# Seven products moved to the front of a stage in a fused retention and feed-forward kernel

## The chip, the cores and the metric

The kernel runs on one core of a Trainium2 chip. The time is device time in microseconds (us) for one execution. Five engines work side by side, each through its own list of instructions in the order in which the program wrote them: TensorE (PE in the profile; its weight loads are PEld), VectorE (DVE), ScalarE (ACT), GpSimd (POOL) and SyncE (SP), which issues most transfers. An instruction that waits holds up all that stand behind it on its engine.

## The reference

A retention layer with a decaying state is followed by a feed-forward layer with a PReLU. In the reference's own words, cut:

```python
gamma = 1.0 - 2.0 ** (-5.0 - np.arange(H))
for t in range(S):                       # B=4, H=8, S=768, D=64
    state = gamma * state + einsum('bhd,bhe->bhde', k[:, :, t], v[:, :, t])
    y[:, :, t] = einsum('bhd,bhde->bhe', q[:, :, t], state) / sqrt(D)
x = y.transpose(0, 2, 1, 3).reshape(3072, 512)
h = x @ w_in                             # 512 x 2048
g = max(h, 0) + alpha * min(h, 0)
out = g @ w_out                          # 2048 x 512, float32
```

## The kernel before

The 3072 tokens are worked in six blocks of 512, numbered 0 to 5, each of two units of 256 tokens. A block has a retention part (scores, masks, outputs, a state handed from unit to unit), a first layer (512 features into 2048, which gives the tile `gt`) and a second layer (2048 into 512). The retention of the next block is written in between the matmuls of the second layer of the present one. Blocks 0 and 1 have first layers of their own (`ffn1`). Blocks 2, 3, 4 and 5 use `ffn1_mixed`, which the change touches.

**The stage `ffn1_mixed` (L396).** The 2048 features are 16 tiles of 128, numbered 0 to 15. Twelve of them (2 to 7 and 10 to 15) are ordinary: four matmuls of 512 columns (L409) into one PSUM bank, then an activation on ACT, `hm = relu(-h)` (L422), and a gate on DVE (L429) that forms `gt = h + (1 - alpha) * hm`. The other four (0, 1, 8 and 9) form group "a" and go through a Winograd form of Strassen's product, with seven products in place of eight. A product is four matmuls of 256 columns (L470). Products 1, 6, 7 and 4 add up in bank 4 (`hx`), products 2, 5 and 3 in bank 5 (`hy`). Between them the results are taken out:

- after product 1, ACT copies bank 4 (copy C1, L483); after product 2, DVE adds that copy to bank 5, which gives C11 (L488);
- after product 6, ACT copies bank 4 (u2); after product 7 it copies it again (u3), and DVE adds u3 to bank 5, with products 2 and 5 in it, which gives C22 (L488);
- after product 4, bank 4 holds C21, which gets one activation on ACT and two half gates of 256 columns on DVE;
- after product 3, DVE adds u2 to bank 5, which gives C12 (L488).

C11, C22 and C12 are gated elsewhere: an activation on ACT (L422, from the sum in SBUF), then a multiplication (L441) and an addition (L447) on POOL. The steps `g11a`, `g22a` and `g12a` of the order string stand for that. A step `s2:5` forms two sums on DVE (L366) over tiles 2 to 4 and 10 to 12 of `gt`, for the second layer; `s5:8` and `s0:2` do it for the rest.

The string `order` (L493) sets the program order on all engines: `n2:7` is tile 2 into bank 7, `p1a` is product 1 with what takes its result out. It is walked by a generator. The loop over the blocks (L873) ticks it: first the rescaling of the next block's q and k for one unit is written (two instructions of 128x1024 on POOL, L156, a transposing transfer and three loads on SP; in block 2 also a cast of v on POOL), then eight ticks, which are two steps of tile or product, then the same for the second unit, eight ticks more, and then the rest. Block 5 has no next block, so none of that.

The tiles `hm`, which hold an activation for the gate, come from a ring of five buffers; `os` (the sums) from a ring of three, `cu` (the copies) from one of four.

**What follows the stage.** `ffn2_seven` (L598) is the second layer, again seven products, each of 16 matmuls of 256 columns (L629). Its first product reads tiles 0 to 7 of `gt` in that order for the block's first 128 tokens, and then again for the next 128; eight ticks after its start the state sums (L219) and the scores (L272) of the next block come in. The scores write banks 4 to 7. Its third product reads the sums of L366. In block 5 nothing comes in between.

Of the kernel before, what the change touches and what calls it, by code (L numbers as in the profile page):

```python
# [21 lines left out]
def kernel(  # L22
# [373 lines left out]
    def ffn1_mixed(n):  # L396
# [89 lines left out]
        def plus(o, t):  # L486
# [4 lines left out]


        order = (  # L493
            "n2:7 n10:2 p1a n3:3 p2a n11:6 g11a p6a n4:1 p5a n12:0 s2:5 p7a n5:7 n13:2 g22a"
            " p4a n6:3 p3a n14:6 g12a n7:1 n15:7 s5:8 s0:2"
        )
        banks = {"a": (4, 5)}
        X, Y, t = {}, {}, {}
# [374 lines left out]
    for n in range(1, NBLK):  # L873
        more = n + 1 < NBLK
        u0 = 2 * (n + 1)
        if n > 1:
            gen = ffn1_mixed(n)
            if more:
                for u in (u0, u0 + 1):
                    i = rescale(G, u, 0, 0, 8)  # L880
                    if u == u0:
                        behind(i, gate)
                    i = rescale(G, u, 1, 0, 8)
                    if u == u0:
                        behind(i, xgate)
                    turn_dma(u)
                    if n == 2:
                        cast_v(G, u)
                    if u + 2 < NU:
                        load(u + 2)  # L890
                    tick(gen, 8)
            tick(gen)
# [68 lines left out]
```

## Time and profile before

| | |
|---|---|
| median of the runs | 211.59 us (211.43 to 212.95, three runs) |
| the profiled execution | 212.18 us, of it the span 210.5 us |
| PE busy | 194.6 us (92%) |
| DVE busy | 167.4 us (80%) |
| ACT busy | 109.1 us (52%) |
| POOL busy | 107.7 us (51%) |
| share of the chain that ended last | PE 57%, DVE 17%, DMA 13% |

Rows of the trace give the start in us from the span's start, the duration in us, the engine, the line of the kernel, the operation, what it writes and reads, the shapes and the count of merged instructions; brackets behind them give the idle time of the engine ahead of the row, and what ended it. Instructions of one engine overlap a little, so the distance of two starts is shorter than a duration.

### The profile page before, as it was taken

The numbers are of one execution on the slowest core, as the hardware profiler recorded it, in microseconds if no ns is written. First come the engines' busy times: TensorE is split into PE (matmuls) and PEld (weight loads), VectorE is DVE, ScalarE is ACT, GpSimd is POOL, SyncE is SP. The second block draws the span as 40 slices with busy tenths as digits, with TensorE's granted clock in tenths as the row PEclk, the third lists the DMA queues.
The fourth block names the chain that finished last, engine by engine and source line by source line (L and its number), as shares of the span: only waits on it lengthen the run. The fifth ranks groups of instructions, "written<-read, shape, count | busy, mean of one in ns | idle before, by whom it ended". The sixth has DMA issues, their size and how long they took to land.

```text
span 210.5 us, 5678 instructions
## 1 busy us (share of the span) xinstructions
PE 194.6 (92%) x2362; PEld 133.1 (63%) x2362; DVE 167.4 (80%) x278; ACT 109.1 (52%) x185; POOL 107.7 (51%) x116
## 2 busy tenths in 40 slices
PE   7789998999999999997899999799998899998993
PEld 2458444584565878554778655688654788654782
DVE  7884985666998997779997679998678997678941
ACT  2376675352666154575275476454486154476221
POOL 2488037750489354985574864573965560045200
PEclk9999999999999999999999999999999999999999
DMA  6999998999986996799411599611650011200004
GB/s 171 342 218 155 185 290 157 278 178 243 311 290 147 272 295 207 195 317 257 120 51 53 167 278 255 203 53 53 186 113 3 0 53 53 100 0 2 18 35 150
DMA packets 64697, 33.95 MB, mean 161 GB/s; under 512 B 18064, under 2 KB 64160, under 8 KB 64672
## 3 DMA queue, kind: packets, MB, share of 16 engines
q1 hardware_dynamic: 60272, 29.37, 48.3%
q0 software_dynamic: 4224, 4.19, 13.3%
q8 instruction: 18, 0.29, 0.6%
q10 hardware_dynamic: 176, 0.03, 0.2%
q14 instruction: 7, 0.06, 0.1%
HBM read 27.30 MB, written 6.29 MB: 160 GB/s over the span
## 4 chain that ended last, share of the span: by engine, by line
PE 57%; DVE 17%; DMA 13%; issue 4%; ACT 3%; POOL 2%; SPq 0%; ACTq 0%; DVEq 0%; POOLq 0%
PE ox L629 14%; PE oy L629 10%; PE hps L409 10%; DVE gt L429 8%; DMA qs<-in_q_dram 5%; PE hps L546 5%; PE ops L581 5%; DMA wout<-in_moe_w_out_dram 4%; DMA win<-in_moe_w_in_dram 4%; DVE gs L366 3%; DVE os L488 2%; ACT hm L422 2%; PE y L317 2%; PE kps L95 2%; PE hy L470 2%
## 5 line engine op out<-in xcount | busy, mean ns | idle before, releaser
L409 PE MATMUL hps<-xT,win 128*128 128x512 f16 x192 | 46.7, 379 | 0.0
L429 DVE SCALAR_TENSOR_TENSOR gt<-hm,oma,hps 128x512 f16<-128x512 f32 x48 | 35.1, 745 | 12.9 <-ACT hm L422 11.9
L422 ACT ACTIVATE hm<-hps 128x512 f32<-128x512 f32 x48 | 27.6, 594 | 15.4 <-PE hps L409 15.4
L629 PEld LDWEIGHTS <-gs 128*128 128x128 f16 x320 | 30.9, 98 | 4.3 <-DVE gs L366 0.4
L559 DVE SCALAR_TENSOR_TENSOR gt<-hm,oma,hps 128x256 f16<-128x256 f32 (+1 forms) x44 | 25.1, 599 | 6.3 <-ACT hm L557 4.4
L629 PEld LDWEIGHTS <-gt 128*128 128x128 f16 x240 | 22.7, 98 | 11.1 <-DVE gt L429 6.8
L409 PEld LDWEIGHTS <-win 128*128 128x128 f16 x192 | 18.8, 98 | 15.8
L546 PE MATMUL hps<-xT,win 128*128 128x256 f16 (+1 forms) x176 | 28.4, 321 | 0.0
L441 POOL TENSOR_TENSOR hm<-hm,oma 128x512 f32<-128x512 f32 x12 | 12.5, 1041 | 28.8 <-ACT hm L422 28.8
L156 POOL TENSOR_TENSOR kdq<-ks,tab 128x1024 f16<-128x1024 f32 (+1 forms) x10 | 17.3, 1728 | 18.6 <-DMA ks<-in_k_dram 8.6
L645 ACT ACTIVATE cu<-ox 128x512 f32<-128x512 f32 (+1 forms) x18 | 9.5, 526 | 28.3 <-PE ox L629 28.3
L557 ACT ACTIVATE hm<-hps 128x512 f32<-128x512 f32 x32 | 19.1, 597 | 9.3 <-PE hps L546 9.3
L156 POOL TENSOR_TENSOR kdq<-qs,tab 128x1024 f16<-128x1024 f32 (+1 forms) x13 | 21.2, 1634 | 5.2 <-DVE xsum L393 4.5
L546 PEld LDWEIGHTS <-win 128*128 128x128 f16 x176 | 17.1, 98 | 10.6
L245 POOL TENSOR_TENSOR tf<-ss,tab 128x256 f32<-128x256 f32 x16 | 12.2, 765 | 16.8 <-DVE ss L244 16.5
L260 POOL CAST tg<-tf 64x256 f16<-64x256 f32 x29 | 14.1, 488 | 11.3 <-DVE tf L241 9.9
L284 DVE TENSOR_TENSOR m<-sca,mi 128x512 f16<-128x512 f32 x24 | 16.4, 685 | 3.7 <-PE scb L272 3.7
L629 PE MATMUL ox<-wsum,gs 128*128 128x256 f16 x160 | 19.1, 273 | 0.1
L335 ACT ACTIVATE xT<-y 128x512 f16<-128x512 f32 x24 | 16.2, 742 | 5.0 <-PE y L317 4.9
L284 DVE TENSOR_TENSOR m<-scb,mi 128x512 f16<-128x512 f32 x24 | 16.4, 681 | 0.0
L366 DVE TENSOR_TENSOR gs<-gt 128x768 f16<-128x768 f16 (+2 forms) x18 | 16.0, 890 | 0.3
L629 PE MATMUL ox<-wout,gt 128*128 128x256 f16 x80 | 10.9, 274 | 5.7 <-DVE gt L429 5.7
(75 smaller groups left out, 307.5 us busy)
## 6 DMA issues: line engine op xcount, KB each, us to landing
out_dram<-os SPq DMA_DIRECT2D x21, 256.0 KB, 2.2
vs<-in_v_dram SPq DMA_DIRECT2D x10, 512.0 KB, 6.6
ks<-in_k_dram SPq DMA_DIRECT2D x8, 512.0 KB, 4.6
qs<-in_q_dram SPq DMA_DIRECT2D x8, 512.0 KB, 5.8
ks<-in_k_dram SPq DMA_DIRECT2D x8, 256.0 KB, 4.5
qs<-in_q_dram SPq DMA_DIRECT2D x8, 256.0 KB, 4.6
win<-in_moe_w_in_dram POOLq DMA_DIRECT2D x4, 512.0 KB, 7.7
wout<-in_moe_w_out_dram POOLq DMA_DIRECT2D x4, 512.0 KB, 8.7
```

Of the source, the lines that this page charges most:

```text
L156: return eng.tensor_tensor(out=kdq[:, t, :, h0:h1, :].rearrange("p r h d -> p h r d"), in0=staged[u]["kq"[t]][:, h0:h1, :].rearrange("p h ...
L260: nc.gpsimd.tensor_copy(out=o, in_=i)
L284: i = nc.vector.tensor_tensor(out=m2, in0=live[u, hh][a].rearrange("p (r a i) -> p r a i", r=2, a=2), in1=mask.unsqueeze(2).to_broadcast([ ...
L335: nc.scalar.activation(out=xT[n][:, ul, :, 128 * c : 128 * c + 128].rearrange("k a (p r) -> k a r p", r=2), in_=ys[c].rearrange("k (a r p) ...
L366: return nc.vector.tensor_tensor(out=o, in0=a, in1=b, op=op)
L409: nc.tensor.matmul(out=hps.rearrange("p (u t) -> p u t", t=U), lhsT=w_in_all[:, hp, 128 * f : 128 * f + 128], rhs=xT[n][:, :, hp, :], star ...
L422: nc.scalar.activation(out=hm, in_=i, func=RELU, bias=0.0, scale=-1.0)
L429: nc.vector.scalar_tensor_tensor(out=gt[:, f, U * lo : U * hi], in0=hm[:, c], scalar=oma_sb[:, f : f + 1], in1=i[:, c], op0=MULT, op1=ADD,)
L546: nc.tensor.matmul(out=hps[:, f, :].rearrange("p (u t) -> p u t", t=U), lhsT=w_in_all[:, hp, 128 * (f0 + f) : 128 * (f0 + f) + 128], rhs=x ...
L557: nc.scalar.activation(out=hm, in_=hps, func=RELU, bias=0.0, scale=-1.0)
L559: nc.vector.scalar_tensor_tensor(out=gt[:, f0 + f, U * lo : U * hi], in0=hm[:, f, :], scalar=oma_sb[:, f0 + f : f0 + f + 1], in1=hps[:, f, :],
L629: nc.tensor.matmul(out=o[1][m], lhsT=lhs(f, m), rhs=rhs(f), start=(first and f == 0 and (m == 0 or o[0] is None)), stop=(f == HF - 1), ski ...
```

## The change

Only the order string is changed. The seven products of group "a" began at the third step, behind tiles 2 and 10, with a tile or two between any two of them. Now product 1 stands first, one tile stands behind each product (two behind product 7), and tiles 6, 14, 7 and 15 are left for the end. The relative orders of the products (1, 2, 6, 5, 7, 4, 3) and of the tiles (2, 10, 3, 11, 4, 12, 5, 13, 6, 14, 7, 15) stay. `g11a` stands behind tile 10 instead of tile 11, `g22a` behind tile 12 instead of tile 13, product 3 behind tile 5 instead of tile 6. `s2:5` stands behind tile 13 instead of tile 12. `g12a` stays between tiles 14 and 7.

```diff
         order = (
-            "n2:7 n10:2 p1a n3:3 p2a n11:6 g11a p6a n4:1 p5a n12:0 s2:5 p7a n5:7 n13:2 g22a"
-            " p4a n6:3 p3a n14:6 g12a n7:1 n15:7 s5:8 s0:2"
+            "p1a n2:7 p2a n10:2 g11a p6a n3:3 p5a n11:6 p7a n4:1 n12:0 g22a p4a n5:7 p3a n13:2"
+            " s2:5 n6:3 n14:6 g12a n7:1 n15:7 s5:8 s0:2"
         )
```

## The prediction

> **What bounds the kernel now.** The page first. TensorE (PE) is busy 92% of the span and VectorE (DVE) 80%; the granted clock, the last line, is 0.998, so throttling takes nothing. So the question is where PE's missing 8% lie. The page's row of the gates (L429) already says that DVE idles 11.9 us ahead of them, for ACT. The columns of the second fence are a stretch, its length, and the busy time (with the count of instructions) of PE, its weight loads, DVE, ScalarE (ACT) and GpSimd (POOL).
>
> ```profile
> span 210.5 us, 5678 instructions
> PE 194.6 (92%) x2362; PEld 133.1 (63%) x2362; DVE 167.4 (80%) x278; ACT 109.1 (52%) x185; POOL 107.7 (51%) x116
> ...
> L429 DVE SCALAR_TENSOR_TENSOR gt<-hm,oma,hps 128x512 f16<-128x512 f32 x48 | 35.1, 745 | 12.9 <-ACT hm L422 11.9
> ...
> core 0: 210.5 us, clock 0.998
> ```
>
> ```profile
> 83.99:100.88 16.89, 14.51 (x86) 7.99 (x83) 13.40 (x20) 10.45 (x19) 13.27 (x11) 1.00 0.97 262
> 116.95:132.72 15.77, 14.36 (x85) 8.02 (x82) 12.28 (x20) 10.45 (x19) 11.11 (x9) 1.00 0.97 260
> 147.96:163.73 15.77, 14.35 (x85) 8.02 (x83) 12.28 (x20) 10.45 (x19) 11.30 (x9) 1.00 0.39 101
> 179.32:195.09 15.77, 14.35 (x85) 8.03 (x83) 12.28 (x20) 10.45 (x19) 5.79 (x6) 1.00 0.10 34
> ...
> 163.73:179.32 15.59, 15.58 (x298) 13.64 (x298) 13.72 (x24) 5.91 (x10) 5.58 (x8) 1.00 0.11 36
> 132.72:147.96 15.24, 15.23 (x294) 13.42 (x295) 14.00 (x24) 6.92 (x10) 7.62 (x11) 1.00 0.25 80
> ```
>
> The first four rows are the stages that the order string governs, blocks 2, 3, 4 and 5, from PE's first tile to the matmul for which PE waits at their end; I call that matmul the restart. Each has about 1.4 us in which PE has nothing. In block 4 (I count t from its start, 147.96):
>
> ```profile
> 147.96 1.89 PE L409 MATMUL hps<-xT,win 128*128 128x512 f16 x8
> 149.68 0.60 PE L470 MATMUL hx<-xT,win 128*128 128x256 f16 x4
> 150.12 1.03 PE L409 MATMUL hps<-xT,win 128*128 128x512 f16 x4
> ...
> 161.38 0.93 PE L629 MATMUL ox<-wout,gt 128*128 128x256 f16 x7
> 163.73 0.28 PE L629 MATMUL ox<-wout,gt 128*128 128x256 f16 x1 [1.42 <-DVE gt L429]
> ```
>
> PE runs without a gap until seven of the eight matmuls of the next product are issued and then waits 1.42 us for a gate on DVE. The gate is that of tile 7. The path to it, on ACT and on DVE:
>
> ```profile
> 149.88 0.60 ACT L422 ACTIVATE hm<-hps 128x512 f32<-128x512 f32 x1 [0.27 <-PE hps L409]
> 150.38 0.59 ACT L483 ACTIVATE cu<-hx 128x512 f32<-128x512 f32 x1
> ...
> 161.78 0.63 ACT L422 ACTIVATE hm<-os 128x512 f32<-128x512 f32 x1 [1.28 <-DVE os L488]
> 162.31 1.07 ACT L422 ACTIVATE hm<-hps 128x512 f32<-128x512 f32 x2
> ```
>
> ```profile
> 156.56 0.56 DVE L366 TENSOR_TENSOR gs<-gt 128x768 f16<-128x768 f16 x1
> 157.15 0.56 DVE L366 TENSOR_TENSOR gs<-gs,gt 128x768 f16<-128x768 f16 x1
> 157.62 0.68 DVE L488 TENSOR_TENSOR os<-hy,cu 128x512 f32<-128x512 f32 x1
> ...
> 159.55 0.87 DVE L429 SCALAR_TENSOR_TENSOR gt<-hm,oma,hx 128x256 f16<-128x256 f32 x2
> 160.34 0.74 DVE L429 SCALAR_TENSOR_TENSOR gt<-hm,oma,hps 128x512 f16<-128x512 f32 x1
> 161.00 0.69 DVE L488 TENSOR_TENSOR os<-hy,cu 128x512 f32<-128x512 f32 x1
> 161.60 0.74 DVE L429 SCALAR_TENSOR_TENSOR gt<-hm,oma,hps 128x512 f16<-128x512 f32 x1
> 162.93 1.41 DVE L429 SCALAR_TENSOR_TENSOR gt<-hm,oma,hps 128x512 f16<-128x512 f32 x2 [0.59 <-ACT hm L422]
> 164.37 0.92 DVE L366 TENSOR_TENSOR gs<-gt 128x768 f16<-128x768 f16 x1
> ```
>
> ACT works in order. C12's activation (161.78) waits 1.28 us for the addition C12 on DVE (161.00), and the activation of tile 7 stands behind it. DVE, behind again, idles 0.59 us before tile 7's gate at 162.93 (t 14.97), and PE restarts 0.80 later (t 15.77).
>
> **The change part by part.** It adds and removes no instruction. It moves products 1, 6, 5, 7, 4, 3 and 2 ahead of tiles, and with them their copies, additions and activations on ACT and DVE, and the pair of sums 2:5 from before tile 5's gate to between the gates of tiles 13 and 6. No DMA is moved, and the four rescales on POOL still stand ahead of C11's multiplication there. So the cost is in how three in-order queues mesh, and I replay them with steps from these rows. PE: a tile 0.86 (two from 147.96 to 149.68), a product 0.44 (149.68 to 150.12). ACT begins 0.20 after PE (149.88 after 149.68), its next instruction 0.50 later, 0.53 behind one that reads SBUF (161.78 to 162.31). DVE begins 0.62 after an activation began (162.31 to 162.93); a gate takes 0.66 (160.34 to 161.00), an addition 0.60, the two half gates of C21 0.79 (159.55 to 160.34), a pair of sums 0.59 + 0.47, and 0.12 for the drain ahead of it (162.93 + 1.41, then 164.37). ACT follows DVE's end by 0.09, and I give it the same behind POOL; POOL begins 0.71 after an activation began (161.78 to 162.49, the row is below).
>
> *Blocks 3, 4 and 5.* PE's sum is the same 13.42, so tile 7 ends at 12.55 as before. ACT starts: copy C1 0.64, tile 2 1.50, tile 10 2.80, C11 3.57, copy 4.11, tile 3 4.59, tile 11 5.40, copy 5.90, tile 4 6.70, tile 12 7.56, C22 8.06, C21 8.60, later tile 14 11.89, C12 12.39, tile 7 12.92. DVE starts: tile 2 2.12, C11 2.78, tile 10 3.42, tile 3 5.21, tile 11 6.02, C22 6.68, tile 4 7.32, tile 12 8.18, and from C21 at 9.22 without a gap: tile 5 10.01, C12 10.67, tile 13 11.27, sums 12.05 and 12.64, tile 6 13.11, tile 14 13.77, tile 7 14.43. PE restarts at 15.23 instead of 15.77. So C12's wait on ACT does go, 1.28 us of it, but **DVE is late next**: tile 7's activation is done by 13.5 and its gate has to queue. The gain is 0.54 a block, the 0.59 of idle time and no more. No product holds up PE: the reader of each bank is done before it is written again, with the smallest margin 0.4 us (C11's addition ends at 3.46, product 5 starts at 3.90).
>
> The sums behind tile 15 gain besides. POOL's rows, with the collision of before:
>
> ```profile
> 151.57 1.91 POOL L156 TENSOR_TENSOR kdq<-qs,tab 128x1024 f16<-128x1024 f32 x1
> ...
> 162.49 1.04 POOL L441 TENSOR_TENSOR hm<-hm,oma 128x512 f32<-128x512 f32 x1 [0.98 <-ACT hm L422]
> 163.60 1.27 POOL L447 TENSOR_TENSOR gt<-hm,os 128x512 f16<-128x512 f32 x1
> ```
>
> The sum of 164.37 took 0.92 against the 0.56 of 156.56: it ended 0.42 after POOL's addition (163.60 + 1.27). After the change POOL runs C12 from 13.10 (ACT's 12.39 + 0.71) to 15.48 (its two steps, 1.11 + 1.27), and that sum starts at 15.87, free. So DVE is 0.36 earlier against the restart. That pays only where PE waits for DVE later on:
>
> ```profile
> 107.56 0.41 PE L317 MATMUL y<-m,vx 64*64 64x128 f16 x15 [0.19 <-DVE m L284]
> 108.48 0.21 PE L272 MATMUL scb<-kq 64*64 64x128 f16 x1 [0.28 <-DVE ss L244]
> ...
> 198.09 1.92 PE L629 MATMUL ox<-wsum,gs 128*128 128x256 f16 x16
> ```
>
> Block 2's second half waits 0.19 + 0.28, of which I take 0.3; block 4's (15.59) is 0.35 longer than block 3's (15.24), which I lay to the same masks on DVE and take as 0.3; block 3's has no such wait. These are bounded by zero and by the full waits. In block 5 the third product starts at 198.09; PE's own work from its restart at 195.09 (25 matmuls at 0.11) ends at 197.84, so 0.25 is won there beside the 0.54.
>
> *Block 2 loses.* POOL also casts v there, and is late:
>
> ```profile
> 95.51 0.60 PE L470 MATMUL hy<-xT,visum 128*128 128x256 f16 x4 [0.96 <-DVE os L488]
> ...
> 95.55 0.63 ACT L422 ACTIVATE hm<-os 128x512 f32<-128x512 f32 x1 [1.67 <-DVE os L488]
> ...
> 91.46 1.04 POOL L441 TENSOR_TENSOR hm<-hm,oma 128x512 f32<-128x512 f32 x1
> 92.58 1.27 POOL L447 TENSOR_TENSOR gt<-hm,os 128x512 f16<-128x512 f32 x1
> ...
> 92.59 1.67 DVE L366 TENSOR_TENSOR gs<-gt 128x768 f16<-128x768 f16 x1
> ```
>
> With t from 83.99, C11's multiplication on POOL starts at 7.47 and ends at 9.86. The buffer of an activation (hm, five in turn) goes again to the fifth activation behind it. Behind C11's that is C22's, in both orders; before, C22's came at 95.55 (t 11.56), 1.7 after POOL's end, held up by DVE. In the new order it would stand at 8.06 on ACT, and waits for POOL until 9.95; behind it wait the activations of C21, tiles 5, 13, 6 and all later ones. In blocks 3 and 4 the same buffer is free at 151.57 + 1.91 + 1.11 + 1.27, t 7.9, under 0.2 ahead of the need. So block 2: C21's activation 10.48, DVE C21 11.10, tile 5 11.89, C12 12.55, tile 13 13.15, first sum 13.93 to 14.49. Meanwhile C22 runs on POOL from 10.66 to 13.04, tile 14's activation has to wait for that buffer (13.13), C12's comes at 13.63, and its multiplication on POOL is ready at 14.34, inside the first sum. What the second sum then does is not in the trace; the bounds are 0.56 if it goes ahead of POOL, and as in row 92.59 (1.67, ending 0.41 after POOL) if POOL gets in between. I take the second: POOL is ready before the second sum is (the collision of the row is with POOL's addition, L447; its multiplication, L441, reads SBUF alike). POOL goes from 14.49 to 15.53, the sum ends at 15.94, then tile 6 15.85, tile 14 16.51, tile 7 17.17, restart 17.97 against 16.89 (100.88): **a loss of 1.08**; by the other bound 17.11, a loss of 0.22. The wait of 0.96 at 95.51 is gone either way, but it lay ahead of the queue that decides.
>
> The Trainium skill (SBUF — State Buffer, "SBUF: two separate sides") says that VectorE and GpSimd share a port pair as an exclusive lock, that the one that starts first keeps it for the whole instruction, and that the other blocks fully. The rows 92.59 and 164.37 agree (0.41 and 0.42 past POOL's end); by it the loss in block 2 is the 1.08.
>
> Sum: -1.08 + 0.3 (block 2), +0.54 (3), +0.54 + 0.3 (4), +0.54 + 0.25 (5) = 1.39 us won. The profiled execution (span 210.5, 212.18 with what lies around it) becomes 210.8; its distance of 0.6 to the median of 211.59 is kept, so the median becomes **210.2**.
>
> **The rivals.** *Second sum free in block 2.* POOL's queue or DVE's is a few tenths off and they miss each other: 0.86 more won, 209.3. For it: the margin is 0.2 us. Against: POOL stands ready first.
>
> *Slower: the moved sums collide in every block.* In blocks 3 to 5 the second sum starts at 12.64 and C12's multiplication on POOL at 13.10, so 0.45 us decide. If DVE is later than that, the sum ends 0.41 after POOL's 1.04, at 14.55 instead of 13.20, tiles 6, 14 and 7 follow at 14.46, 15.12 and 15.78, and PE restarts at 16.58, 0.8 late. Three times 0.8 and block 2's 0.8 give 3.2 lost, 214.8; if one or two blocks escape, some 213. Against it: DVE's queue from C21 on is only the rows' own steps. For it: C22's activation in blocks 3 and 4 has just 0.2 us to its buffer, and a slip there moves DVE alone.
>
> *The change does not do what it says.* DVE's idle time, 0.59 before tile 7, comes back elsewhere, since DVE now waits 1.1 us for tile 3's activation behind C11's, and the bound was DVE's sum all along. Then blocks 3 to 5 win nothing, block 2 loses 0.8, and the time is 212.4.
>
> **How the numbers follow.** Forecast 0.45 (209.9 to 210.9 by the bounds of the later waits), second sum free 0.18, nothing won 0.18, collisions everywhere 0.16, and 0.03 for what I don't see. The range 209.1 to 213.3 leaves out most of the collisions and a little at the lower end. One per cent, about what a measurement here can tell from no change, is 2.1 us: faster by over that (below 209.5) is most of the second case and a tail of the first, 0.16; slower (above 213.7) is most of the collisions, 0.14; within it 0.70.
>
> **What would show it.** In blocks 3 to 5 PE's last wait, 1.42 now, should fall to 0.9, with no wait of ACT's C12 activation for DVE, and DVE's queue unbroken from C21 on. In block 2 that wait should rise to about 3.5, C22's activation should wait some 1.9 us for POOL, and one sum of 128x768 should take about 1.4. The last sums should take 0.56, not 0.92. A long sum in blocks 3 to 5 as well, or a wait of PE for C11's or C22's addition, would make the prediction wrong.

## The result, and the profile after

The changed kernel takes 210.55 us (median of 20 runs, 209.27 to 212.54) against 211.82 for the kernel before (20 runs, 211.16 to 213.40). The ratio is 0.9921, with a 95% interval of 0.9898 to 0.9945: 0.8% faster. This ratio leaves out two runs of the changed kernel as slow (212.45 and 212.54 us), although their low clock of 0.983 is probably the change's own doing, as the experiments below suggest; the two medians as they stand differ by 0.6%. The profiled execution took 210.19 us, its span 208.5.

From the page of the changed kernel: the span, the busy times, the clock that was granted to PE in 40 slices of the span, and the gates.

```profile
span 208.5 us, 5674 instructions
PE 195.7 (94%) x2362; PEld 134.1 (64%) x2362; DVE 166.9 (80%) x278; ACT 109.5 (53%) x185; POOL 107.6 (52%) x116
...
PEclk9999999999999999999789999999999999999999
...
L429 DVE SCALAR_TENSOR_TENSOR gt<-hm,oma,hps 128x512 f16<-128x512 f32 x48 | 34.7, 743 | 9.6 <-ACT hm L422 8.9
```

DVE's idle time ahead of the gates, 12.9 us before, is the sum over all blocks and says little yet. The clock has a hole that was not there before: slices 20 and 21 show 7 and 8 tenths. The stages come next, as stretches; the columns are those of the prediction's second fence, and the third number from the end is the granted clock. First the four stages of the order string, from product 1 to the restart (the first half of a block), then the second halves of blocks 2 to 5, from the restart on. The last row is of the kernel before: the second half of its block 2.

```profile
83.21:100.89 17.68, 14.56 (x86) 8.03 (x83) 12.96 (x20) 10.34 (x19) 14.57 (x11) 1.00 0.98 267
117.67:132.75 15.08, 14.35 (x86) 8.03 (x83) 12.18 (x20) 10.56 (x19) 11.64 (x9) 1.00 0.96 259
147.88:162.96 15.08, 14.35 (x85) 8.04 (x83) 12.17 (x20) 10.56 (x19) 11.66 (x9) 1.00 0.41 105
178.30:193.38 15.08, 14.35 (x85) 8.01 (x83) 12.17 (x20) 10.56 (x19) 6.46 (x6) 1.00 0.10 35
...
100.89:117.67 16.78, 16.78 (x309) 14.17 (x310) 13.84 (x25) 7.86 (x12) 7.34 (x11) 0.90 0.10 34
132.75:147.88 15.13, 15.13 (x293) 13.36 (x294) 13.33 (x24) 6.92 (x10) 7.20 (x11) 1.00 0.29 93
162.96:178.30 15.34, 15.34 (x297) 13.57 (x298) 13.42 (x24) 5.90 (x10) 4.89 (x8) 1.00 0.11 36
193.38:208.50 15.12, 11.64 (x105) 10.19 (x105) 7.51 (x11) 3.07 (x8) 0.47 (x1) 0.98 0.20 70
...
100.88:116.95 16.07, 15.59 (x309) 13.54 (x310) 14.20 (x25) 7.63 (x12) 8.44 (x12) 1.00 0.17 54
```

| block | first half, predicted | measured | second half, predicted | measured |
|---|---|---|---|---|
| 2 | 1.08 lost | 0.79 lost (16.89 to 17.68) | 0.3 won | 0.71 lost (16.07 to 16.78) |
| 3 | 0.54 won | 0.69 won (15.77 to 15.08) | 0 | 0.11 won (15.24 to 15.13) |
| 4 | 0.54 won | 0.69 won | 0.3 won | 0.25 won (15.59 to 15.34) |
| 5 | 0.54 won | 0.69 won | 0.25 won | 0.29 won (15.41 to 15.12) |

From the start of block 2 on that is 1.22 us won, where 1.39 was forecast. The span is 2.0 shorter; the other 0.78 lies ahead of block 2 (which starts at 83.21 instead of 83.99), in code that the change does not touch. Block 2 started anywhere between 83.2 and 85.0 in this study's profiles of kernels with the same work ahead of it, so that part belongs to the single execution.

PE's rows at the ends of the stages of blocks 2, 3 and 4:

```profile
96.67 0.82 PE L629 MATMUL ox<-wout,gt 128*128 128x256 f16 x6
99.57 0.28 PE L629 MATMUL ox<-wout,gt 128*128 128x256 f16 x1 [2.08 <-DVE gt L429]
100.89 0.28 PE L629 MATMUL ox<-wout,gt 128*128 128x256 f16 x1 [1.03 <-DVE gt L429]
...
132.75 0.28 PE L629 MATMUL ox<-wout,gt 128*128 128x256 f16 x1 [0.73 <-DVE gt L429]
...
162.96 0.28 PE L629 MATMUL ox<-wout,gt 128*128 128x256 f16 x1 [0.73 <-DVE gt L429]
```

In blocks 3 and 4 the wait ahead of the restart fell from 1.42 to 0.73 us (0.9 was forecast). In block 2 it rose to 2.08 + 1.03 with one matmul in between (3.5 was forecast). The queues of block 4, ACT's and then DVE's:

```profile
155.94 0.62 ACT L422 ACTIVATE hm<-os 128x512 f32<-128x512 f32 x1
...
160.35 0.62 ACT L422 ACTIVATE hm<-os 128x512 f32<-128x512 f32 x1
160.87 1.23 ACT L422 ACTIVATE hm<-hps 128x512 f32<-128x512 f32 x2
```

```profile
157.08 0.87 DVE L429 SCALAR_TENSOR_TENSOR gt<-hm,oma,hx 128x256 f16<-128x256 f32 x2 [0.26 <-ACT hm L422]
...
159.13 0.74 DVE L429 SCALAR_TENSOR_TENSOR gt<-hm,oma,hps 128x512 f16<-128x512 f32 x1
159.79 0.55 DVE L366 TENSOR_TENSOR gs<-gt 128x768 f16<-128x768 f16 x1
160.37 0.56 DVE L366 TENSOR_TENSOR gs<-gs,gt 128x768 f16<-128x768 f16 x1
160.85 2.71 DVE L429 SCALAR_TENSOR_TENSOR gt<-hm,oma,hps 128x512 f16<-128x512 f32 x4
163.60 0.56 DVE L366 TENSOR_TENSOR gs<-gt 128x768 f16<-128x768 f16 x1
```

With t from 147.88, C22's activation comes at 8.06 (replayed: 8.06), C21's half gates at 9.20 (9.22), the second sum at 12.49 (12.64). C12's activation no longer waits for DVE, and from C21 on DVE has no gap: the four gates of 160.85, tile 7's the third of them, simply queue. The second sum ends at 160.93, 0.12 before POOL's multiplication of C12 begins (161.05). The last sums take 0.56 (163.60; it was 0.92). In block 2 the queues look otherwise:

```profile
93.08 0.63 ACT L422 ACTIVATE hm<-os 128x512 f32<-128x512 f32 x1 [1.71 <-POOL gt L447]
...
96.22 0.60 ACT L422 ACTIVATE hm<-hps 128x512 f32<-128x512 f32 x1 [0.56 <-POOL gt L447]
```

```profile
91.78 1.26 POOL L447 TENSOR_TENSOR gt<-hm,os 128x512 f16<-128x512 f32 x1
...
97.41 1.04 POOL L441 TENSOR_TENSOR hm<-hm,oma 128x512 f32<-128x512 f32 x1 [1.23 <-ACT hm L422]
```

```profile
97.52 1.34 DVE L366 TENSOR_TENSOR gs<-gs,gt 128x768 f16<-128x768 f16 x1
```

C22's activation waits 1.71 us for POOL's addition of C11 (91.78 + 1.26), tile 14's waits 0.56 for that of C22, and the second sum collides with C12's multiplication on POOL (97.41): 1.34 us, ending at 98.86, 0.41 after POOL. All of that was forecast. What was not is the clock behind it:

```profile
102.00:104.00 2.00, 2.00 (x30) 1.37 (x19) 1.93 (x6) 0.00 (x0) 0.13 (x1) 0.50 0.00 0
...
102.40:106.60 4.20, 4.20 (x30) 3.15 (x27) 3.98 (x10) 1.07 (x3) 1.40 (x3) 0.65 0.01 4
```

From 102.00 to 104.00 PE had half of its clock (the half clock, below), and over the 4.2 us from 102.40 on 0.65 of it on average.

### The profile page after: what moved, and what is told of

Same layout as the page of the kernel before. It is cut to its first block, busy times and chain, and to the rows that moved or that the text cites. A ratio compares the mean times of both kernels' runs of the same rounds, so it can differ in the third digit from the quotient of the medians.

```text
span 208.5 us, 5674 instructions
## 1 busy us (share of the span) xinstructions
PE 195.7 (94%) x2362; PEld 134.1 (64%) x2362; DVE 166.9 (80%) x278; ACT 109.5 (53%) x185; POOL 107.6 (52%) x116
## 4 chain that ended last, share of the span: by engine, by line
PE 66%; DVE 16%; POOL 7%; issue 5%; ACT 4%; POOLq 0%; DVEq 0%; ACTq 0%
PE hps L546 13%; PE ox L629 13%; PE oy L629 10%; DVE gt L429 8%; PE hps L409 7%; PE ops L581 6%; DVE gs L366 4%; PE kps L95 3%; POOL kdq L156 3%; PE hx L470 3%; PE y L317 2%; PE sca L272 2%; ACT hm L422 2%; DVE m L284 2%; PE y L302 2%
## 5 line engine op out<-in xcount | busy, mean ns | idle before, releaser
L409 PE MATMUL hps<-xT,win 128*128 128x512 f16 x192 | 46.0, 379 | 0.0
L422 ACT ACTIVATE hm<-hps 128x512 f32<-128x512 f32 x48 | 28.2, 596 | 10.9 <-PE hps L409 10.2
L629 PEld LDWEIGHTS <-gt 128*128 128x128 f16 x240 | 23.4, 101 | 11.7 <-DVE gt L429 6.6
L557 ACT ACTIVATE hm<-hps 128x512 f32<-128x512 f32 x32 | 19.1, 597 | 9.4 <-PE hps L546 9.3
L156 POOL TENSOR_TENSOR kdq<-qs,tab 128x1024 f16<-128x1024 f32 (+1 forms) x13 | 20.4, 1573 | 6.2 <-DVE xsum L393 5.2
L629 PE MATMUL ox<-wout,gt 128*128 128x256 f16 x80 | 12.0, 288 | 5.3 <-DVE gt L429 5.3
L447 POOL TENSOR_TENSOR gt<-hm,os 128x512 f16<-128x512 f32 x12 | 15.4, 1285 | 0.9
```

What stands on the lines that cost most here:

```text
L156: return eng.tensor_tensor(out=kdq[:, t, :, h0:h1, :].rearrange("p r h d -> p h r d"), in0=staged[u]["kq"[t]][:, h0:h1, :].rearrange("p h ...
L409: nc.tensor.matmul(out=hps.rearrange("p (u t) -> p u t", t=U), lhsT=w_in_all[:, hp, 128 * f : 128 * f + 128], rhs=xT[n][:, :, hp, :], star ...
L422: nc.scalar.activation(out=hm, in_=i, func=RELU, bias=0.0, scale=-1.0)
L447: nc.gpsimd.tensor_tensor(out=gt[:, f : f + 2, U * j : U * j + U], in0=hm, in1=i.rearrange("p (f t) -> p f t", f=2), op=ADD,)
L557: nc.scalar.activation(out=hm, in_=hps, func=RELU, bias=0.0, scale=-1.0)
L629: nc.tensor.matmul(out=o[1][m], lhsT=lhs(f, m), rhs=rhs(f), start=(first and f == 0 and (m == 0 or o[0] is None)), stop=(f == HF - 1), ski ...
```

## The experiments

Ten kernels, each timed beside the kernel before on the same chip; the ratios are to that. Theory A is the prediction's account, with the half clock added as a consequence of PE's long pause in block 2. Waits and pauses are those of each kernel's one profiled run.

### Seven buffers for the activations

```diff
-            hm = sbp.tile([128, TB], FP, tag="hm", bufs=5, name="hm")
+            hm = sbp.tile([128, TB], FP, tag="hm", bufs=7, name="hm")
```

It stands at both places that make an `hm`, L421 and L555.

> The changed kernel with seven buffers for hm in place of five. Theory A (the ring of hm behind POOL's late start costs block 2 its 2.6 us, and PE's long wait there brings the half clock behind it): C22's activation in block 2 does not wait for POOL, that stage lasts 15.1 us like the others (17.68 now), the clock stays at 1.00 after it, blocks 3 to 5 do not change; 207.0 us, 3.5 under the changed kernel. Rival B (POOL itself, late by the casts, is what block 2 waits for, whatever the buffers): the stage stays over 17, 210.5. Rival C (the ring costs the wait, but the half clock comes without it): 208.

207.68 us (six runs, 207.02 to 209.35), ratio 0.9819 (0.9777 to 0.9861). First and second half of block 2, and the first half of block 3:

```profile
83.19:98.80 15.61, 14.52 (x86) 8.01 (x83) 12.22 (x20) 10.57 (x19) 14.49 (x11) 1.00 0.95 253
98.80:114.50 15.70, 15.42 (x310) 13.51 (x311) 13.83 (x25) 7.63 (x12) 7.51 (x12) 1.00 0.27 86
114.50:129.57 15.07, 14.34 (x85) 8.00 (x82) 12.12 (x20) 10.57 (x19) 11.79 (x9) 1.00 0.96 253
```

Block 2's first half fell from 17.68 to 15.61, its second from 16.78 to 15.70 at full clock, block 3 stayed. Rivals B and C fall: the ring is what made block 2 slow, and without the pause there was no half clock (0.998 or more in all six runs). The 0.5 us to the other blocks remained: one activation still waited 0.72 us for POOL. Here the second sum began 0.06 us ahead of POOL's multiplication of C12 (96.21 and 96.27); it took its usual 0.56, and the multiplication took 1.40 instead of 1.04.

### Eight buffers

```diff
-    tab = sbp.tile([128, 96], FP, tag="tab", name="tab")
+    tab = sbp.tile([128, 52], FP, tag="tab", name="tab")
...
-    warm = sbp.tile([128, 128], FP, tag="warm", name="warm")[:, 0:1]
-    oma_sb = sbp.tile([128, 128], FP, tag="oma", name="oma")[:, 0:NFT]
+    warm = sbp.tile([128, 8], FP, tag="warm", name="warm")[:, 0:1]
+    oma_sb = sbp.tile([128, 16], FP, tag="oma", name="oma")[:, 0:NFT]
...
-            hm = sbp.tile([128, TB], FP, tag="hm", bufs=5, name="hm")
+            hm = sbp.tile([128, TB], FP, tag="hm", bufs=8, name="hm")
```

> The changed kernel with eight buffers for hm, and three small constant tiles cut to what is used of them, to make room. With seven, block 2's first half still lasted 15.61 us, since there tile 5's activation, the seventh behind C11's, waited 0.72 for POOL. Theory A (the ring is all that is left of block 2's loss): with eight no activation waits for POOL there, the first half lasts 15.1 as in the other blocks, and the time is 0.5 under that with seven, 207.2. Rival J (C12's multiplication on POOL still meets the second sum of block 2, whatever the ring): 15.6 stays, 207.7.

Eight is what there is room for: with nine, and the three small tiles as they were, the kernel's tiles need 210.875 kB of a partition of SBUF, and 207.874 are there. The start and the restart of block 2:

```profile
85.03 0.60 PE L470 MATMUL hx<-xT,win 128*128 128x256 f16 x4
...
100.26 0.28 PE L629 MATMUL ox<-wout,gt 128*128 128x256 f16 x1 [0.89 <-DVE gt L429]
```

The first half of block 2 is 15.23 us (85.03 to 100.26), so with the ring out of the way hardly anything of block 2's loss is left, and rival J falls. The half microsecond that theory A expected of the whole time does not show: 207.81 (206.93 to 208.55), ratio 0.9798 (0.9762 to 0.9833), cannot be told from the time with seven. These two are the fastest versions seen.

### Seven buffers for the kernel before

> The kernel before with seven buffers for hm. Theory A: no activation waits there for POOL, so nothing changes, 211.8 us. Rival E (the ring of five binds the old order too, unseen): 0.5 us faster or more.

212.03 us (12 runs), ratio 1.0004 (0.9977 to 1.0030). Nothing: the ring binds in the new order alone, and rival E falls.

### Product 3 alone moved

```diff
-            " p4a n6:3 p3a n14:6 g12a n7:1 n15:7 s5:8 s0:2"
+            " p4a p3a n6:3 n14:6 g12a n7:1 n15:7 s5:8 s0:2"
```

This is the kernel before with one product moved past one tile.

> The kernel before with product 3 alone moved, ahead of tile 6, so that the addition C12 stands ahead of tile 6's gate on DVE. Theory A (what blocks 3 to 5 gain is C12's addition coming off the path of tile 7's activation): PE stands 0.87 us at product 3, for C22's addition, but the restart comes 0.5 to 0.6 earlier in blocks 3 to 5, the wait ahead of it falls to about 0, and the time is 209.7 to 210.3. Rival D (the gain needs the products in front, which make DVE's queue dense): restart as before or later, 211.8 to 212.5.

209.60 us (208.89 to 210.05), ratio 0.9890 (0.9856 to 0.9924). Block 3, which starts at 116.16, on PE:

```profile
126.56 0.60 PE L470 MATMUL hy<-xT,visum 128*128 128x256 f16 x4 [0.72 <-DVE os L488]
...
130.45 1.20 PE L629 MATMUL ox<-wout,gt 128*128 128x256 f16 x8
```

PE stands 0.72 us at product 3 (0.87 was expected; in block 2 it is 1.81), and then issues all eight matmuls of the next product without a wait; the eighth starts at about 131.21 (130.45 and seven steps of 0.11), t 15.05. The whole change reaches 15.08. So the restart of blocks 3 to 5 needs none of the six other products, and rival D falls. The time is 0.1 under what was expected. Behind the restart the two differ: the second halves of blocks 3 to 5 last 15.38, 15.73 and 15.55 us here, and 15.13, 15.34 and 15.12 with the whole change.

### Product 3 alone put back

The changed kernel with seven buffers, so that block 2 doesn't cover the result:

```diff
-            "p1a n2:7 p2a n10:2 g11a p6a n3:3 p5a n11:6 p7a n4:1 n12:0 g22a p4a n5:7 p3a n13:2"
-            " s2:5 n6:3 n14:6 g12a n7:1 n15:7 s5:8 s0:2"
+            "p1a n2:7 p2a n10:2 g11a p6a n3:3 p5a n11:6 p7a n4:1 n12:0 g22a p4a n5:7 n13:2"
+            " s2:5 n6:3 p3a n14:6 g12a n7:1 n15:7 s5:8 s0:2"
```

> The changed kernel with seven buffers for hm, and product 3 alone put back behind tile 6, as the kernel before has it. Theory A (C12's place decides the restart): C12's activation waits for DVE again with tile 7's behind it, the restart falls back to 15.7 or 15.8 in blocks 3 to 5 (15.08), PE's wait ahead of it to 1.4, and the time rises from 207.7 to some 210. Rival H (the gain of blocks 3 to 5 is that of the six other products in front): restart and time stay, 207.7.

212.28 us (10 runs), ratio 0.9994 (0.9967 to 1.0021): the whole gain is gone, more than expected. ACT's row of C12 and PE's restart in block 3 (from 117.21):

```profile
131.01 0.63 ACT L422 ACTIVATE hm<-os 128x512 f32<-128x512 f32 x1 [1.32 <-DVE os L488]
```

```profile
101.14 0.28 PE L629 MATMUL ox<-wout,gt 128*128 128x256 f16 x1 [2.16 <-DVE gt L429]
...
132.97 0.28 PE L629 MATMUL ox<-wout,gt 128*128 128x256 f16 x1 [1.41 <-DVE gt L429]
```

C12's activation waits 1.32 us for DVE again, PE 1.41, and the restart is at 15.76. In block 2 the pause was 2.16 us, and five of the ten runs had a mean clock of 0.990 or 0.991. That is a small part of what the time lies above 210, since the runs at full clock took 211.6 us or more too. The profiled run shows the rest: beside the 0.7 in each first half of blocks 3 to 5, block 2's first half lasts 16.50 instead of 15.61, and the second halves of blocks 2 to 5 are 0.37, 0.08, 0.24 and 0.27 longer than with seven buffers alone. Rival H falls. Together with the last experiment: C12's place alone is enough for the restart, and without it the other moves gain nothing.

### The sums back behind tile 12

```diff
-            "p1a n2:7 p2a n10:2 g11a p6a n3:3 p5a n11:6 p7a n4:1 n12:0 g22a p4a n5:7 p3a n13:2"
-            " s2:5 n6:3 n14:6 g12a n7:1 n15:7 s5:8 s0:2"
+            "p1a n2:7 p2a n10:2 g11a p6a n3:3 p5a n11:6 p7a n4:1 n12:0 s2:5 g22a p4a n5:7 p3a n13:2"
+            " n6:3 n14:6 g12a n7:1 n15:7 s5:8 s0:2"
```

> The changed kernel with the sums 2:5 back behind tile 12, ahead of tile 5's gate. Theory A (DVE's 16-bit sums and POOL's instructions keep one another out, multiplication as well as addition): in blocks 3 to 5 the first sum meets C22's multiplication on POOL and the second its addition, they take 1.3 and 1.6 us in place of 0.56, and PE restarts 1.3 to 1.5 later; in block 2 C12's multiplication meets no sum, and the restart comes 1.5 earlier; together 212 to 213.5 us. Rival G (POOL's multiplication does not block a sum, only its addition does): at most 0.5 lost in blocks 3 to 5, 209 to 210.

212.21 us (12 runs), ratio 1.0018 (0.9990 to 1.0045). Block 3's sums, and POOL's work on C22:

```profile
124.40 1.23 DVE L366 TENSOR_TENSOR gs<-gt 128x768 f16<-128x768 f16 x1
125.67 1.51 DVE L366 TENSOR_TENSOR gs<-gs,gt 128x768 f16<-128x768 f16 x1
```

```profile
124.18 1.04 POOL L441 TENSOR_TENSOR hm<-hm,oma 128x512 f32<-128x512 f32 x1 [1.11 <-ACT hm L422]
125.30 1.46 POOL L447 TENSOR_TENSOR gt<-hm,os 128x512 f16<-128x512 f32 x1
```

The first sum ran 1.23 us, to 0.41 after the multiplication's end (124.18 + 1.04); the second 1.51, to 0.42 after the addition's. POOL's addition, ready during the first sum, took 1.46 instead of 1.27. Restarts: block 3 at 16.48 (1.40 later), block 2 at 15.85 (1.83 earlier).

```profile
83.79:99.64 15.85, 14.57 (x86) 8.02 (x83) 12.99 (x20) 10.35 (x19) 13.65 (x11) 1.00 0.95 264
115.42:131.90 16.48, 14.68 (x85) 8.02 (x83) 13.80 (x20) 10.57 (x19) 11.87 (x9) 1.00 0.99 267
```

Multiplication and addition both hold a sum up; rival G falls. So the new place of the sums, which I had seen as a risk, is what saves blocks 3 to 5 from a loss of 1.4 us each, and it costs block 2.

### The sums behind tile 15

The changed kernel with seven buffers, and

```diff
-            " s2:5 n6:3 n14:6 g12a n7:1 n15:7 s5:8 s0:2"
+            " n6:3 n14:6 g12a n7:1 n15:7 s2:5 s5:8 s0:2"
```

> The changed kernel with seven buffers for hm and the sums 2:5 behind tile 15, with the other sums. Theory A (what holds tile 7's gate after the change is DVE's queue, 1.2 us of it these sums): the restart comes 0.7 earlier in every block and PE's wait ahead of it is about 0, the sums are still ready for the third product of blocks 2 to 4 and 0.9 late in block 5; 205.5 to 206.5 us. Rival F (DVE's total decides, and the time is given back at the masks of the second half): 207.5, as with seven buffers alone.

209.10 us (208.81 to 209.92), ratio 0.9873 (0.9836 to 0.9910), so 1.4 slower than with seven buffers alone (1.1 by the ratios, each taken on its own chip), and not faster as theory A had it. Block 2's halves, and two of PE's waits, in the second half of block 2 and in block 5:

```profile
83.73:98.28 14.55, 14.35 (x86) 8.02 (x83) 11.19 (x18) 10.57 (x19) 13.43 (x11) 1.00 0.94 249
98.28:115.19 16.91, 15.62 (x310) 13.62 (x310) 15.03 (x27) 7.63 (x12) 8.20 (x12) 1.00 0.32 99
```

```profile
105.79 0.41 PE L317 MATMUL y<-m,vx 64*64 64x128 f16 x15 [1.00 <-DVE m L284]
...
195.17 1.92 PE L629 MATMUL ox<-wsum,gs 128*128 128x256 f16 x16 [1.16 <-DVE gs L366]
```

The restart came at 14.55 (0.7 under 15.08 was expected), but PE then waited 1.00 us at the masks and 1.16 at the third product of block 5. What is taken off DVE's queue ahead of the restart comes back behind it, with interest: rival F was right in kind, and the loss was more than it said.

### The casts moved to ACT

```diff
-                    if n == 2:
-                        cast_v(G, u)
...
-            if n > 1 and u0 + 2 < NU:
+            if u0 + 2 < NU:
                 cast_v(A, u0 + 2)
```

The same for `u0 + 3`; the ring has five buffers.

> The changed kernel, hm with five buffers, but the two casts of v that POOL does at the start of block 2 done by ACT in block 1's second layer, as the later blocks have it. Theory A (POOL's lateness behind those casts holds the buffer): C22's activation in block 2 finds its buffer free, that stage lasts 15.1 us (17.7), no half clock, 207.0 to 207.7 us if the casts cost ACT nothing there. Rival B (the ring alone, or something else in block 2): the wait for POOL stays, 210.5.

210.64 us (12 runs), ratio 0.9926 (0.9894 to 0.9958). The stretch ahead of block 2, and block 2's first half:

```profile
82.23:87.39 5.16, 5.16 (x32) 3.99 (x32) 2.20 (x5) 1.77 (x3) 2.32 (x2) 0.67 0.29 102
87.39:102.47 15.08, 14.34 (x86) 8.02 (x83) 12.18 (x20) 10.56 (x19) 9.77 (x8) 1.00 0.93 240
```

```profile
80.64 1.06 ACT L170 ACTIVATE vx<-vs 128x1024 f16<-128x1024 f32 x1 [3.10 <-DMA vs<-in_v_dram]
...
82.23 2.41 PE L629 MATMUL ox<-wsum,gt 128*128 128x256 f16 x16 [2.34 <-ACT cu L645]
```

Block 2's first half is 15.08 us, exactly as in the other blocks: POOL's lateness is the cause of the wait for the ring. But on ACT the cast waits 3.10 us for its load, PE's operand stands behind it, and PE pauses 2.34 us ahead of block 2. The next 5.16 us ran at a clock of 0.67. The stall moved, and the half clock with it; that the time is the one rival B named is chance.

### Idle matmuls in block 2's pause

```diff
+        if n == 2:
+            keep(9, 5)
         gen = ffn2_seven(n, 0, 1) if more else ffn2_seven(n, (0, 3), 1, 2)
```

> The changed kernel with nine matmuls of 512 columns, whose result nobody reads, ahead of block 2's second layer: 1.94 us of work laid into PE's wait of 3.1 us, ending before the gate of tile 6 comes. Theory A (the pause in block 2 brings the half clock): no half clock behind block 2 in any run, clock 1.00, 209.5 us. Rival C (the clock falls by chance or by PE's load): dips in most runs as before, 210.5 us.

209.30 us (208.96 to 210.84), ratio 0.9891 (0.9855 to 0.9926), with a clock of 0.997 or more in all six runs.

```profile
83.51:101.19 17.68, 16.50 (x95) 8.88 (x92) 12.96 (x20) 10.34 (x19) 14.58 (x11) 1.00 0.96 253
101.19:116.88 15.69, 15.41 (x309) 13.52 (x310) 13.81 (x25) 7.63 (x12) 7.28 (x11) 1.00 0.16 53
```

The first half is 17.68 as without them, the second 15.69 instead of 16.78. PE had nine matmuls more to do ahead of it, and the second half was 1.09 us shorter; with seven buffers and with the casts on ACT it lasts 15.70 too. Rival C falls.

With four idle matmuls (`keep(4, 5)`):

> The changed kernel with four idle matmuls in block 2's pause in place of nine: 0.86 us of work, so the pauses behind it are about 1.2 and 1.0 us in place of 2.1 and 1.0. Theory A (the half clock comes of the long pause alone, and single pauses up to 1.8 us were seen without it): no half clock, as with nine, 209.3. Rival I (any two pauses that add up to some 2 us bring it): dips in half of the runs or more, 210 to 210.5.

210.23 us (209.46 to 213.51), ratio 0.9908 (0.9872 to 0.9944); the pauses were 1.22 and 1.03, and two of six runs had a mean clock of 0.989 and 0.992, four had 1.00. That lies between the two expectations; with six runs, it stays open where the limit lies.

The pauses in or near block 2, in the profiled run, and the clock, over all timed runs whose clock is on record:

| kernel | PE's longest pauses, us | runs with a mean clock under 0.995 |
|---|---|---|
| before | 0.96; 1.42 | 0 of 68 |
| nine idle matmuls | at most 1.03 | 0 of 6 |
| product 3 alone moved | 1.81 | 0 of 6 |
| four idle matmuls | 1.22, one matmul, 1.03 | 2 of 6 |
| product 3 put back | 2.16 | 5 of 10 |
| casts on ACT | 2.34 | 9 of 12 |
| the change | 2.08, one matmul, 1.03 | 15 of 20 |

The five other kernels, with pauses of at most 1.40 us, had no such run in 42. Of the changed kernel's 20 runs the five at full clock have a median of 209.75, the other fifteen 210.76; the five lowest clocks among these, 0.983, go with a median of 212.04.

## Why the prediction was right, and where it was not

**The time.** 210.2 was forecast and 210.55 measured, inside the range of 209.1 to 213.3, and 0.8% is on the "within 1%" side that had 0.70.

**Blocks 3 to 5: mechanism right, size low by a quarter.** 0.54 a block was forecast from the replay, 0.69 measured. The term that was off is one: "0.12 for the drain ahead" of a pair of sums. Behind tile 13, whose gate these sums do not read, there is no such gap. The same shows with the sums behind tile 15, which they do not read either: the first of them (130.16) starts 0.09 before that gate ends. In block 4 the first sum starts 0.66 after that gate (159.13, 159.79), at 11.91 instead of 12.05, and the second sum, tile 6 and the restart (15.08 instead of 15.23) are early by the same 0.14 or 0.15. That DVE would be late next, that its queue would have no gap from C21 on, and that the sums would miss POOL is what the rows show. The step "the 0.59 of idle time and no more" was too tight for the same reason: the drain goes too.

**Which part of the change does it.** The prediction put the gain down to C12's wait and did not say what the six other products bring. The runs do: product 3 alone reaches the same restart (15.05 and 15.08), and everything but product 3 reaches 15.76, which is the kernel before. The rival "the change does not do what it says" was wrong: blocks 3 to 5 did gain. The other moves are not worthless, though. Behind the restart they win 0.25, 0.39 and 0.43 us in blocks 3, 4 and 5 against product 3 alone, and with seven buffers the whole change is 1.9 us faster than product 3 alone with five (207.68 and 209.60 us, on one chip). With five buffers block 2 takes that gain away. Which of the other moves brings it no run separates, and product 3 alone with seven buffers was not tried (in its profile with five, no activation waits for POOL).

**Block 2, first half: right.** The ring, C22's wait for POOL and the second sum's collision all came as replayed; 1.08 was forecast and 0.79 measured: the second sum ended at t 15.65 (98.86) instead of 15.94, because POOL's multiplication began at 14.20 and not at 14.49. It was ready 0.14 earlier, and the first sum, for which the replay had it wait 0.15, was all but over, again for want of the drain. (The 9.86 that the prediction gives for the end of C11's multiplication is the end of its addition, which is what the buffer waits for.) The rival with a free second sum did not occur. The Trainium skill's rule (SBUF — State Buffer, "SBUF: two separate sides") had decided for the collision, and the runs bear it out: a sum that met a running POOL instruction ended 0.41 to 0.43 us after it, and a sum that began first, with seven buffers, held POOL up instead (1.40 for 1.04).

**Block 2, second half: wrong.** The step "of which I take 0.3" reckoned with later waits and not with the clock. The waits did shrink: with the idle matmuls the half takes 15.69 against 16.07, 0.38 won. But PE's pause, 2.08 and 1.03 us with one matmul in between, which the prediction itself had worked out (3.5), cost 1.09 in the profiled run by a clock of one half, and the mean clock was under 0.995 in fifteen runs of twenty (where in those the hole lies, only the profiled one shows). The prediction had said of the clock only that it takes nothing before, and did not ask whether the pause that it forecast would change that. The Trainium skill has a rule for it (TensorE: Matmul & The Clock Gate, "Part 1: The HAM clock gate"): after an idle window of about 3.4 us the clock falls to half, and some 3.4 us of work bring it back. The runs agree in kind. In size, less was enough here: a single pause of 2.34 us in nine runs of twelve, and one of 2.16 in five of ten.

That the sum came so near, 1.22 for 1.39, is luck in part, since the errors cancelled: the first halves came out 0.74 us better than forecast, and block 2's second half 1.01 worse. By the profiles, the change without the half clock would have won some 2.3 us from block 2 on (an estimate, 1.22 + 1.09); the five runs at full clock are 2.1 us under the kernel before.

## What to carry to other kernels

Replay in-order queues step by step from the trace's own distances, and the order of events comes out to a few tenths; then look through the replay for the two things that it creates anew, a ring of buffers that comes round to a late engine, and a pause of the matmul engine long enough to cost it its clock. A change that moves many things is best tried in its smallest part as well: here one product past one tile gave as much as the whole change, and what the rest could give showed only once the ring was longer. And a tile that holds intermediate results for two engines wants as many buffers as the later engine lags: two more made 0.8% into 1.8%.

## What the runs showed of the hardware

The clock falls after shorter pauses of PE than I had in mind, in some runs and not in others of the same kernel: 2.2 to 2.3 us of pause gave it in half to three quarters of the runs, one of up to 1.8 in none of 80 runs of the table (two of 1.2 and 1.0 close together in two of six). Laying work that nobody reads into such a pause made the kernel faster by about a microsecond. And POOL's two-operand instructions and DVE's 16-bit sums hold one another up, by who starts first: each sum that met a running one ended 0.41 to 0.43 us after it, and a POOL multiplication that began 0.06 after a sum took 1.40 us instead of 1.04.
